# Reordering the ScalarE work of a ramp phase: log/exp of the third unit before the exponentials of the second

## The chip, the cores and the metric

The kernel runs on one core of a Trainium2 chip. The metric is the device time of one execution in microseconds (us). A program on one core has no second die to compare with, so a run is called slow only when it is more than 1.5% above the fastest run of the same kernel.

Engines are named as the profile names them: PE is TensorE (PEld is its weight load), ACT is ScalarE, DVE is VectorE, POOL is GpSimd. "Clock" is the clock that was granted to TensorE: 1.0 is full, 0.5 is half.

## The reference

Two operators follow each other. The first is a gated linear recurrence (a complex decay per channel, D = 48, 8 heads, 4 batches, 768 steps), the second a GEGLU layer with a gated residual on the 3072 tokens that result (384 channels, 1536 hidden).

```python
mag = np.sqrt(a_re * a_re + a_im * a_im)
scale = np.minimum(mag, 0.999) / (mag + 1e-06)
a_re_n, a_im_n = (a_re * scale, a_im * scale)
for t in range(S):                      # S_re, S_im: [B, H, D, D]
    new_re = ar * S_re - ai * S_im
    new_im = ar * S_im + ai * S_re
    S_re, S_im = (new_re + kv, new_im)  # kv = outer(k[t], v[t])
    y[:, :, t] = np.einsum('bhd,bhde->bhe', q[:, :, t], S_re)
# ... x = y with the heads side by side
g = x @ w_gate
gelu = 0.5 * g * (1.0 + erf(g * inv_sqrt2))
ffn_out = gelu * (x @ w_val) @ w_out
return x + 1.0 / (1.0 + np.exp(-(x @ w_res))) * ffn_out
```

The kernel does not step through time. It takes the logarithm of the magnitude and the angle of each decay, forms cumulative sums over 128 tokens by matmuls with triangular matrices, turns them into exponentials (E and its inverse Ei) and sines and cosines (CS), multiplies q and k by these, and so turns the recurrence into causal attention over 128-token blocks plus a carried state.

## The kernel before

The 3072 tokens are 12 groups of 256 (4 batches of 3), and the groups form units: [0], [1,2], [3,4], ... The program alternates between a phase x (log/exp, exponentials, arctan, sines, half of the attention) and a phase y (Gelu and the GEGLU matmuls, the other half of the attention). The program puts a table load on ACT where it changes between the log/exp functions, the trigonometric ones and Gelu; the trace of before has 21 such loads of 1.28 us each. The change is in phase x of unit 0. There "the second unit" is g1 = groups 1 and 2, "the third unit" is g2 = groups 3 and 4.

```python
def p1_steps(g):                        # log/exp of one group
    def s0():
        act(out=T["lm", g], in_=T["lm", g], func=AF.Ln)
    def s1():
        T["s", g] = pS.tile([128, W], FP, tag="s", name="s")          # pS: 2 buffers
        act(out=T["s", g], in_=T["lm", g], func=AF.Exp, scale=-1.0)
        nc.vector.tensor_tensor(out=T["th", g], in0=T["s", g], in1=T["th", g], op=OP.mult)
    def s2():
        act(out=T["s", g], in_=T["th", g], func=AF.Square)
    def s3():
        act(out=T["s", g], in_=T["s", g], func=AF.Ln, bias=1.0)
        # ... two DVE updates of lm
    return [s0, s1, s2, s3]

def cs_l(g, c):                         # cumulative sum of log magnitudes
    cs = psM.tile([128, DM], FP, tag="mm", padded_shape=[128, 512], name="csl")   # psM: 4 PSUM slots
    nc.tensor.matmul(out=cs, lhsT=lmat[c], rhs=T["lm", g][:, sl], start=True, stop=True)
    def ex():
        act(out=T["E", g][:, sl], in_=cs, func=AF.Exp)
        act(out=T["Ei", g][:, sl], in_=cs, func=AF.Exp, scale=-1.0)
    return ex

def cs_t(g, c):                         # cumulative sum of the angles
    if c == 0:
        T["fg", g] = pE.tile([128, C * H, 2, D], FP, tag="fg", name="fg")         # pE: 2 buffers
    cs = psM.tile([128, DM], FP, tag="mm", padded_shape=[128, 512], name="cst")
    nc.tensor.matmul(out=cs, lhsT=tmat[c], rhs=th[:, sl], start=True, stop=(s == 0))
    if s > 0:
        nc.tensor.matmul(out=cs, lhsT=ones2pi, rhs=T["P", g], start=False, stop=True)
    # ... fractions r, fg on DVE; p2_sin then makes CS from fg on ACT

def sums(g):                            # decay between groups
    ms = psM.tile([128, H], FP, tag="mm", padded_shape=[128, 512], name="ms")
    two = pS.tile([128, W], FP, tag="s", name="two")
    # ... two = lm of the last half group + lm of this one, each head twice (DVE)
    for h in range(H):
        nc.tensor.matmul(out=ms[0:DD, h:h + 1], lhsT=two[:, h * DD:(h + 1) * DD], rhs=ones1,
                         start=(h == 0), stop=(h == H - 1), skip_group_check=True)
    T["ms", g] = mp.tile([128, H], FP, tag="ms", name="msb")
    nc.vector.tensor_copy(out=T["ms", g][0:DD], in_=ms[0:DD])

def sums_exp(g):
    act(out=M[0:DD], in_=T["ms", g][0:DD], func=AF.Exp)
```

Phase x weaves its lists of steps: every list gets a begin and an end, and the steps are emitted in order of their positions. ACT's table-bound functions keep the order in which they are emitted.

```python
weave((0.0, 0.25, zip_steps([p1(g) for g in g1])), (0.26, 0.3, csls), (0.31, 0.32, sm[0]), (0.35, 0.45, exs),
      (0.4, 0.64, zip_steps([p1(g) for g in g2])), (0.641, 0.642, dec3), (0.645, 0.65, atn[:1]),
      (0.65, 0.66, [call(p1_arctan, g) for g in g1]), (0.67, 0.85, cst), (0.75, 0.8, atn[1:]),
      (0.9, 0.95, sin), (0.96, 0.97, sm[1]), (0.0, 0.5, att))
```

Here `sm[0]` are the sums of the second unit, `exs` its exponentials, `dec3` the exponentials M of the sums, `atn[:1]` the table load for arctan, `sm[1]` the sums of the third unit, and `att` the attention of unit 0.

## Time and profile before

| reading | before |
|---|---|
| time, median of 3 runs | 323.64 us (323.56 to 323.77) |
| span of the profiled run | 322.4 us |
| PE busy over the span | 272.1 us (84%) |
| ACT table load that ends log/exp | starts at 48.05 us |
| angle matmuls (cst) | from 50.24 us to the next instruction of PE at 57.51 us |
| first Gelu | 65.02 us |

These lines are from the page of before. The first gives busy time and share of the span by engine. In the other two each digit is the busy share, or the granted clock, of one fortieth of the span (8.06 us) in tenths.

```profile
PE 272.1 (84%) x2200; PEld 170.5 (53%) x2200; DVE 234.8 (73%) x431; ACT 209.8 (65%) x353; POOL 80.5 (25%) x115
...
PE   0337927789887999789997999998999999899994
...
PEclk9995676959999999999999999999999999999998
```

From the ninth slice on PE is busy for 70% or more of every slice but the last, so most of a delay there should go into the end time. Before that the slices have a different limit, which the timeline shows. The columns of the timeline are: start in us, duration in us, engine, line, operation, out<-in with shapes, number of merged instructions, and in brackets the idle time before it with what ended it. ACT of before:

```profile
36.59 0.49 ACT L124 ACTIVATE E<-csl 128x384 f32<-128x384 f32 x1 [0.91 <-PE csl L212]
...
40.92 0.48 ACT L399 CAST x<-y 128x384 bf16<-128x384 f32 x1 [0.55 <-PE y L396]
...
48.05 1.28 ACT L477 ACT_TABLE_LOAD   x1
...
57.58 0.94 ACT L124 ACTIVATE CS<-fg,hpi 128x768 bf16<-128x768 f32 x1 [5.20 <-DVE fg L246]
...
65.02 0.66 ACT L124 ACTIVATE h<-gp 128x256 bf16<-128x256 f32 x2
```

PE of before, in the same view:

```profile
39.21 1.44 PE L296 MATMUL ms<-ones,two 128*96 128x1 f32 x16
...
40.72 1.50 PE L296 MATMUL ms<-ones,two 128*96 128x1 f32 x16
50.24 1.65 PE L236 MATMUL cst<-ai,lt0b 128*128 128x384 f32 x2 [7.84 <-ACT ai L124]
51.68 1.49 PE L238 MATMUL cst<-P,ones2pi 128*128 128x384 f32 x2
...
57.51 1.44 PE L296 MATMUL ms<-ones,two 128*96 128x1 f32 x16
```

And DVE of before:

```profile
47.13 0.96 DVE L197 SCALAR_TENSOR_TENSOR ar<-s,ar 128x768 f32<-128x768 f32 x1 [1.64 <-ACT s L124]
...
50.54 0.54 DVE L224 TENSOR_TENSOR P<-ai 128x384 f32<-128x384 f32 x1
...
51.94 0.94 DVE L293 TENSOR_TENSOR two<-ar 128x768 f32<-128x768 f32 x1
...
59.53 0.95 DVE L321 TENSOR_TENSOR Q<-CS,qE 128x1536 bf16<-128x1536 bf16 x1
```

Read together, they say what limits the stretch from 36 to 65 us. PE waits 7.84 us for the arctan (`ai`), which follows the table load, which follows the last log/exp work of ACT. Then ACT waits 5.20 us for the angle fractions `fg`, which follow the cst matmuls. The way to an earlier Gelu is an earlier table load, followed by cst matmuls that need not wait for P.

The windows view gives the length of a stretch, the busy time (and number of instructions) of PE, PEld, DVE, ACT and POOL in it, then the granted clock, the DMA share and GB/s. Two stretches of before:

```profile
54.00:58.00 4.00, 4.00 (x18) 2.40 (x16) 3.29 (x8) 0.42 (x1) 0.00 (x0) 0.96 1.62 155
...
66.00:71.00 5.00, 5.00 (x41) 4.18 (x40) 3.07 (x8) 1.74 (x4) 1.03 (x2) 0.50 0.75 146
```

By windows of 0.4 us (all clock times below are read so, and are good to 0.4 us) the clock of before is half from 44.0 to 54.4 us and again from 64.8 to 71.6 us.

### The profile page before, as it was taken

To read this page: it belongs to the slowest core of one execution; us is meant where nothing else is said; L and a number is where in the kernel's file an instruction comes from. 1 tells how busy PE (TensorE), PEld (TensorE's weight loads), DVE (VectorE), ACT (ScalarE), POOL (GpSimd) and SP (SyncE) were. 2 spreads that over 40 slices of the span, in tenths; PEclk is the share of its full clock that TensorE was granted. 3 is DMA by queue.
4 is the path that set the end of the run, shared out by engine and by line. 5 is a ranking of instruction groups with operands and counts; after the bars stand their busy time and mean duration, and the time that the engine had idled before them with its cause. 6 is when DMAs were issued, how large, how long until landed. Compare 5 with 4: busy or idle time off the path is not lost.

```text
span 322.4 us, 5853 instructions
## 1 busy us (share of the span) xinstructions
PE 272.1 (84%) x2200; PEld 170.5 (53%) x2200; DVE 234.8 (73%) x431; ACT 209.8 (65%) x353; POOL 80.5 (25%) x115
## 2 busy tenths in 40 slices
PE   0337927789887999789997999998999999899994
PEld 0116624677543666445664556554656655555682
DVE  2446769968499995599982999974899837864352
ACT  4549684646998557977568976569665683656150
POOL 1206522022040370259020572000630003200220
PEclk9995676959999999999999999999999999999998
DMA  8999999989999995396850595000360003600441
GB/s 159 218 183 181 182 169 165 185 174 180 187 179 186 223 160 33 76 197 113 122 36 2 107 121 95 2 0 3 75 122 3 2 0 76 122 2 0 107 91 50
DMA packets 137755, 34.55 MB, mean 107 GB/s; under 512 B 126848, under 2 KB 137728, under 8 KB 137728
## 3 DMA queue, kind: packets, MB, share of 16 engines
q1 hardware_dynamic: 103296, 23.60, 36.8%
q0 software_dynamic: 34432, 10.59, 31.2%
q8 instruction: 17, 0.28, 0.3%
q14 instruction: 10, 0.08, 0.1%
HBM read 31.31 MB, written 9.07 MB: 125 GB/s over the span
## 4 chain that ended last, share of the span: by engine, by line
PE 56%; SPq 12%; ACT 11%; DMA 9%; DVE 6%; issue 3%; POOL 1%; ACTq 0%; DVEq 0%; POOLq 0%
PE vp L443 14%; PE gp L439 13%; SPq L136 6%; SPq L144 6%; PE op L463 6%; DMA k<-in_k_dram 4%; PE rp L455 3%; PE tp L349 3%; PE tp L346 3%; PE at L356 3%; ACT L477 3%; DMA m<-dm 3%; ACT s L124 3%; PE cst L236 2%; PE y L394 2%
## 5 line engine op out<-in xcount | busy, mean ns | idle before, releaser
L124 ACT ACTIVATE h<-gp 128x512 bf16<-128x512 f32 (+1 forms) x84 | 44.5, 536 | 38.4 <-PE gp L439 37.9
L439 PE MATMUL gp<-xT,wg 128*128 128x512 bf16 (+1 forms) x252 | 65.4, 353 | 3.4 <-ACT h L124 2.0
L443 PE MATMUL vp<-xT,wv 128*128 128x512 bf16 (+1 forms) x252 | 66.6, 353 | 0.0
L446 DVE SCALAR_TENSOR_TENSOR h<-h,vp 128x512 bf16<-128x512 bf16 (+1 forms) x84 | 49.8, 603 | 16.4 <-PE vp L443 12.0
L463 PE MATMUL op<-wo,h 128*128 128x384 bf16 x288 | 50.2, 326 | 8.1 <-ACT Ei L124 5.9
L463 PEld LDWEIGHTS <-h 128*128 128x128 bf16 x288 | 27.8, 98 | 28.7 <-issue 11.3
L351 ACT COPY qk<-tp 96x512 bf16<-96x512 bf16 x48 | 27.9, 580 | 17.1 <-PE tp L349 7.9
L359 DVE TENSOR_TENSOR atm<-at,mask 128x512 bf16<-128x512 f32 x48 | 32.9, 686 | 8.2 <-PE at L356 7.8
L472 POOL DMA_DIRECT2D out_dram<-x x22 | 20.4, 947 | 54.4 <-DMA out_dram<-ot 43.1
L439 PEld LDWEIGHTS <-wg 128*128 128x128 bf16 x252 | 23.7, 99 | 17.9 <-issue 4.2
L443 PEld LDWEIGHTS <-wv 128*128 128x128 bf16 x252 | 23.8, 99 | 13.3
L189 DVE TENSOR_TENSOR ai<-s,ai 128x768 f32<-128x768 f32 x12 | 11.1, 955 | 23.6 <-ACT s L124 23.6
L477 ACT ACT_TABLE_LOAD x21 | 26.9, 1283 | 1.1 <-PEq L615 0.7
L346 PE MATMUL tp<-ident,Q 128*96 128x128 bf16 x192 | 20.1, 231 | 6.9 <-DVE Q L321 6.2
L346 PEld LDWEIGHTS <-Q 128*96 128x96 bf16 x192 | 17.4, 130 | 15.3 <-DVE Q L321 10.0
L124 ACT ACTIVATE CS<-fg,hpi 128x768 bf16<-128x768 f32 x12 | 11.2, 935 | 20.8 <-DVE fg L246 20.7
L150 POOL DMA_DIRECT2D v<-in_v_dram x24 | 21.9, 932 | 4.2 <-DMA v<-in_v_dram 1.3
L349 PE MATMUL tp<-ident,K 128*96 128x128 bf16 x192 | 22.3, 235 | 0.0
L236 PE MATMUL cst<-ai,lt0b 128*128 128x384 f32 x24 | 11.8, 577 | 11.7 <-ACT ai L124 11.0
L352 DVE COPY qk<-tp 96x512 bf16<-96x512 bf16 x48 | 19.8, 413 | 2.3 <-ACT qk L351 1.7
L212 PE MATMUL csl<-ar,lt0a 128*128 128x384 f32 x24 | 11.4, 562 | 10.8 <-DMA ar<-in_a_re_dram 10.8
L466 DVE SCALAR_TENSOR_TENSOR ot<-sg,op 128x384 f32<-128x384 f32 x24 | 13.1, 547 | 10.1 <-PE op L463 10.1
(85 smaller groups left out, 522.0 us busy)
## 6 DMA issues: line engine op xcount, KB each, us to landing
ar<-in_a_re_dram SPq DMA_DIRECT2D x24, 192.0 KB, 4.7
ai<-in_a_im_dram SPq DMA_DIRECT2D x24, 192.0 KB, 4.1
q<-in_q_dram SPq DMA_DIRECT2D x24, 192.0 KB, 3.8
k<-in_k_dram SPq DMA_DIRECT2D x24, 192.0 KB, 3.7
out_dram<-ot SPq DMA_DIRECT2D x24, 192.0 KB, 2.5
out_dram<-x POOLq DMA_DIRECT2D x22, 192.0 KB, 3.7
v<-in_v_dram POOLq DMA_DIRECT2D x24, 96.0 KB, 5.0
wg<-in_moe_w_gate_dram POOLq DMA_DIRECT2D x4, 288.0 KB, 11.4
```

Of the source, the lines that this page charges most:

```text
L124: tab(nc.scalar.activation(**kw))
L150: nc.gpsimd.dma_start(out=t[:, c], in_=rows(v, g, c))
L346: nc.tensor.transpose(out=tp[0:DD, j * 128:j * 128 + 128], in_=Q(x), identity=ident)
L349: nc.tensor.transpose(out=tp[0:DD, 512 + j * 128:640 + j * 128], in_=K(x), identity=ident)
L351: nc.scalar.copy(out=qk[0:DD, 0:512], in_=tp[0:DD, 0:512])
L359: nc.vector.tensor_tensor(out=atm, in0=at, in1=mask4, op=OP.mult)
L439: nc.tensor.matmul(out=gp, lhsT=wg[:, fi, ffi * 128:(ffi + 1) * 128], rhs=xT[:, fi, :], start=(fi == 0), stop=(fi == KD - 1))
L443: nc.tensor.matmul(out=vp, lhsT=wv[:, fi, ffi * 128:(ffi + 1) * 128], rhs=xT[:, fi, :], start=(fi == 0), stop=(fi == KD - 1))
L446: nc.vector.scalar_tensor_tensor(out=h2[:, ffi, :], in0=h2[:, ffi, :], scalar=0.5, in1=vp, op0=OP.mult, op1=OP.mult)
L463: nc.tensor.matmul(out=ps, lhsT=h2[:, ffi, jj * 128:(jj + 1) * 128], rhs=wo[:, ffi, :], start=(ffi == 0), stop=(ffi == KF - 1))
L472: nc.gpsimd.dma_start(out=out[t0:t0 + 128, :], in_=T["x", token(u, jj)], accum_op=OP.add)
L477: tab(nc.scalar.preload_act_table_set(nm))
```

## The change

The intent is to let ACT start the third unit's log/exp chain (Ln, Exp, Square, Ln, with a DVE product in the middle) before the second unit's eight exponentials, so that the exponentials fill the waits for DVE and the last Ln is reached sooner. No instruction is added or removed.

`two` must leave the ring "s". Otherwise the third unit's Exp would need a buffer that is held by `two`, which is read by matmuls that wait for a PSUM slot, which is freed by exponentials that now stand behind that Exp on ACT. (This is read from the code.) It goes to the ring "fg" of pE, which has two buffers and is otherwise used for the angle fractions.

```diff
-        two = pS.tile([128, W], FP, tag="s", name="two")
+        two = pE.tile([128, C * H, 2, D], FP, tag="fg", name="two").rearrange("p x u d -> p (x u d)")[:, 0:W]
@@
-            weave((0.0, 0.25, zip_steps([p1(g) for g in g1])), (0.26, 0.3, csls), (0.31, 0.32, sm[0]), (0.35, 0.45, exs),
-                  (0.4, 0.64, zip_steps([p1(g) for g in g2])), (0.641, 0.642, dec3), (0.645, 0.65, atn[:1]),
+            p12 = zip_steps([p1(g) for g in g2])
+            weave((0.0, 0.25, zip_steps([p1(g) for g in g1])), (0.26, 0.3, csls), (0.31, 0.32, sm[0]), (0.32, 0.5, p12[:-2]),
+                  (0.5, 0.58, exs), (0.6, 0.64, p12[-2:]), (0.641, 0.642, dec3), (0.645, 0.65, atn[:1]),
```

## The prediction

> **What bounds the kernel now.** On the whole PE: 272 us busy of 322 (84%), and from 72 us on TensorE is 88 to 100% busy in most 8-us windows. The change touches only the ramp's phase from about 23 to 65 us, where PE is not the limit: in the timeline it is idle from 42.4 to 50.2 us (7.84 us, "released by ACT ai"). The limit there is a loop ACT -> DVE -> ACT -> PE: exponentials 36.6 to 42.2, log/exp of the third unit interleaved and ended at 47.8, table load 48.05 (1.28 us), arctan 49.34, cumulative-sum matmuls 50.24 to 57.5, sines 57.6 to 62.7, first Gelu at 65.0. ACT's waits between 32.6 and 48.05 add up to only about 4 us.
>
> **What the change does.** It adds and removes no work, only order and a buffer.
> 1. ACT: two Ln (0.84 us), two Exp, two Square go ahead of the eight exponentials E/Ei (0.48 us each, 0.38 apart). The Ln fill the 0.84-us and 0.5-us waits after 32.6. But both squares wait for DVE's two products, which stand behind attention and sum instructions to about 41.3, so some waits only move. By the durations of the trace I get the table load at about 47.2 instead of 48.05: 0.8 to 1.1 us earlier.
> 2. DVE: the E/Ei now end near 45.3 instead of 42.2. The ones-column sums (ms) wait for PSUM buffers that E/Ei free, so they start near 43 instead of 39.2; the copies msb, qE, xT and kE stand behind them on DVE, and behind these the log-magnitude updates and the carry P. I expect that update at 47.5 to 48.6 instead of 47.13, P at 51 to 52 instead of 50.54, and the second sum matmul, which needs P, at 51.5 to 52.6 instead of 51.68. That eats the gain of step 1.
> 3. The buffer of "two" moves from the s ring to the fg ring (else the Exp of the third unit would wait for sums that wait for exponentials behind it on ACT). So the third "two" must wait for both sines of the first group (to about 59.4), and TensorE's ms behind it, then gate/value matmuls, Q, K. I expect Q 1 to 3 us later than 59.5, K likewise, first Gelu 64 to 67 (before 65.02).
> 4. TensorE clock. The windows view shows 0.5 from 44 to 54 and from 64.6 to 71.3 us, in steps of about 3.4 us; matmuls there take twice as long. [...] With sums and gate/value matmuls moved later, the slow stretch around 64.6 can shift, shorten or lengthen: an estimated -2 to +1.5 us.
>
> **Sum.** Steps 1 to 3: first Gelu from -1 to +2 us, mid +0.8. Step 4: mid -0.6. What is left at 72 us goes through nearly whole, because PE is dense afterwards. I predict 323.8 us, 322.2 to 325.8 for 8 in 10. Over 2% either way would need 6.5 us: 1% each.
>
> **What would show it.** Step 1: last table load before arctan starts at 47 to 47.5. Step 2: ms starts after 42.5; DVE's first update of the third unit not before 47.3; idle of PE before the second sum matmul. Step 3: "two" in the 58-to-61 stretch with ACT CS as its releaser, and ms behind it. Step 4: the windows view of granted clock from 54 to 74.
>
> **What would make it wrong.** The clock staying full from 54 us on (then 321 to 322); the sums not delaying DVE because the clock is still full at 43 to 46; or the delayed Q and K of the second unit cascading through attention into the following phase (then 326).

+0.8 us for steps 1 to 3 and -0.6 us for step 4 on the 323.63 us of before give the 323.8 us. The -2 to +1.5 us of step 4 is the estimate for the slow stretch that the windows view shows there (0.5 from 64.6 to 71.3 us, in steps of about 3.4 us), not a measured figure. That matmuls take about twice as long there can be read from PE's records of before: cst matmuls start 640 ns apart at half clock (51.0 to 54.2 us) and 322 to 323 ns apart at full clock (54.6 to 57.2 us).

## The result

| reading | before | changed |
|---|---|---|
| time, median of 4 runs | 323.63 us (323.56 to 323.77) | 327.41 us (326.99 to 328.52) |
| span of the profiled run | 322.4 us | 325.1 us |
| ratio of fast runs | 1 | 1.0122 (95%: 1.0094 to 1.0149) |

A ratio is the mean time of one kernel's fast runs over the mean of the other's of the same rounds, so it is not quite the ratio of the medians in the table. The changed kernel is slower, by less than 2%. The same kernel was measured again later, on the second of the three chips of the experiments, where it was 0.7% slower (below). The page of the changed kernel:

```profile
PE 274.0 (84%) x2175; PEld 173.8 (53%) x2200; DVE 233.9 (72%) x431; ACT 209.3 (64%) x353; POOL 80.3 (25%) x115
...
PE   0336876699977999789998899998989999899995
...
PEclk9955655859999999999999999999999999999999
```

The busy times are within 2 us of those of before, PEld's within 3.3 us (25 of PE's records are missing in this trace). The work is the same; it stands later. ACT of the changed kernel:

```profile
39.66 0.48 ACT L399 CAST x<-y 128x384 bf16<-128x384 f32 x1 [3.30 <-PE y L396]
...
41.91 0.47 ACT L124 ACTIVATE E<-csl 128x384 f32<-128x384 f32 x1
...
48.74 0.21 ACT L124 ACTIVATE M<-msb 96x8 f32<-96x8 f32 x1 [2.16 <-DVE msb L299]
48.96 1.28 ACT L477 ACT_TABLE_LOAD   x1
...
60.69 0.94 ACT L124 ACTIVATE CS<-fg,hpi 128x768 bf16<-128x768 f32 x1 [7.39 <-DVE fg L246]
...
68.88 0.66 ACT L124 ACTIVATE h<-gp 128x256 bf16<-128x256 f32 x2
```

PE of the changed kernel:

```profile
42.81 2.72 PE L296 MATMUL ms<-ones,two 128*96 128x1 f32 x16 [3.19 <-ACT Ei L124]
45.78 2.72 PE L296 MATMUL ms<-ones,two 128*96 128x1 f32 x16 [0.25 <-DVE msb L299]
...
51.15 1.65 PE L236 MATMUL cst<-ai,lt0b 128*128 128x384 f32 x2 [2.31 <-ACT ai L124]
53.56 1.65 PE L238 MATMUL cst<-P,ones2pi 128*128 128x384 f32 x2 [0.77 <-DVE P L224]
...
60.08 0.81 PE L238 MATMUL cst<-P,ones2pi 128*128 128x384 f32 x2
...
63.50 1.49 PE L296 MATMUL ms<-ones,two 128*96 128x1 f32 x16 [2.61 <-DVE two L293]
```

DVE of the changed kernel:

```profile
48.54 0.16 DVE L299 COPY msb<-ms 96x8 f32<-96x8 f32 x1 [1.91 <-PE ms L296]
...
50.02 0.95 DVE L197 SCALAR_TENSOR_TENSOR ar<-s,ar 128x768 f32<-128x768 f32 x1
...
52.96 0.55 DVE L224 TENSOR_TENSOR P<-ai 128x384 f32<-128x384 f32 x1
...
62.39 0.96 DVE L293 TENSOR_TENSOR two<-ar 128x768 f32<-128x768 f32 x1 [0.21 <-ACT CS L124]
...
65.11 0.94 DVE L321 TENSOR_TENSOR Q<-CS,qE 128x1536 bf16<-128x1536 bf16 x1
```

And the same two stretches in the windows view:

```profile
54.00:58.00 4.00, 4.00 (x7) 2.08 (x7) 2.31 (x5) 0.00 (x0) 0.00 (x0) 0.50 1.52 152
...
66.00:71.00 5.00, 4.36 (x36) 3.71 (x35) 4.35 (x8) 2.35 (x5) 1.93 (x3) 0.50 0.99 193
```

The reader should follow one chain through these lines.

1. The sums `ms` need a PSUM slot that an exponential frees. The exponentials now start at 41.91 instead of 36.59 us, so the first sum starts at 42.81 instead of 39.21 us ("3.19 <-ACT Ei").
2. By then the clock is half (0.50 in the windows view from 42.0 us). Sixteen one-column matmuls take 2.72 instead of 1.44 us. The second sum starts only when DVE has copied out the first ("0.25 <-DVE msb"); it seems to get the first one's PSUM slot. The second copy is done at 48.70 us.
3. M, the exponential of the sums, stands ahead of the table load on ACT. It waits 2.16 us for that copy, and the table load behind it starts at 48.96 instead of 48.05 us. ACT was otherwise idle for these 2.16 us, and the load did not pass.
4. DVE's updates and P stand behind the same copy. P starts at 52.96 instead of 50.54 us, and the second cst matmul waits for it (0.77 us).
5. The clock stays half until 58.8 instead of 54.4 us.

The cst matmuls therefore end 3.2 us later. Their end is read as the start of the next instruction that was ready: PE's `ms` at 57.51 us of before; in the changed kernel the last two start at 60.08 us, and two such matmuls take 0.65 us at full clock (pairs of before start at 54.93, 55.57, 56.22 and 56.86 us), which gives 60.73 us. This delay of 3.22 us has three terms: the first cst matmul is 0.91 us later (51.15 - 50.24); from the first to the second it took 2.41 instead of 1.44 us, which is 0.97 us for P; and the rest, 1.34 us, is the longer half-clock stretch (without the wait, the eight matmuls took 8.61 instead of 7.27 us).

Then the buffer comes in. The third unit's `two` waits in the fg ring for the sines (62.39 instead of 51.94 us), PE is idle for 2.61 us before its sums, and Q is at 65.11 instead of 59.53 us. The first Gelu is 3.86 us later (68.88 instead of 65.02), the table load that ends the next phase y 3.1 us later (86.61 instead of 83.52), and the whole span 2.7 us longer.

### The profile page after: what moved, and what is told of

The parts are those of the page before. It is cut to its first block, busy times and chain, and to the rows that moved or that the text cites. A ratio compares the mean times of both kernels' runs of the same rounds, so it can differ in the third digit from the quotient of the medians.

```text
span 325.1 us, 5825 instructions
## 1 busy us (share of the span) xinstructions
PE 274.0 (84%) x2175; PEld 173.8 (53%) x2200; DVE 233.9 (72%) x431; ACT 209.3 (64%) x353; POOL 80.3 (25%) x115
## 4 chain that ended last, share of the span: by engine, by line
PE 48%; SPq 15%; DMA 12%; ACT 10%; DVE 8%; issue 4%; POOL 1%; ACTq 0%; DVEq 0%; POOLq 0%
PE gp L439 12%; PE vp L443 12%; SPq L136 10%; PE op L463 5%; SPq L144 5%; DMA q<-in_q_dram 4%; PE rp L455 4%; ACT s L124 3%; PE tp L346 3%; PE tp L349 3%; DMA m<-dm 3%; PE at L356 3%; ACT L477 2%; PE y L394 2%; PE dk L386 2%
## 5 line engine op out<-in xcount | busy, mean ns | idle before, releaser
L439 PE MATMUL gp<-xT,wg 128*128 128x512 bf16 (+1 forms) x241 | 63.7, 352 | 2.9 <-DVE xT L430 1.2
L443 PE MATMUL vp<-xT,wv 128*128 128x512 bf16 (+1 forms) x238 | 61.8, 350 | 0.3
L359 DVE TENSOR_TENSOR atm<-at,mask 128x512 bf16<-128x512 f32 x48 | 33.0, 687 | 10.4 <-PE at L356 9.9
L472 POOL DMA_DIRECT2D out_dram<-x x22 | 20.0, 928 | 54.8 <-DMA out_dram<-ot 54.4
L477 ACT ACT_TABLE_LOAD x21 | 26.9, 1283 | 1.1 <-PEq L616 0.7
L394 PEld LDWEIGHTS <-atm 128*128 128x128 bf16 x192 | 12.6, 97 | 14.1 <-DVE atm L359 12.7
```

The source lines that it names most:

```text
L359: nc.vector.tensor_tensor(out=atm, in0=at, in1=mask4, op=OP.mult)
L439: nc.tensor.matmul(out=gp, lhsT=wg[:, fi, ffi * 128:(ffi + 1) * 128], rhs=xT[:, fi, :], start=(fi == 0), stop=(fi == KD - 1))
L443: nc.tensor.matmul(out=vp, lhsT=wv[:, fi, ffi * 128:(ffi + 1) * 128], rhs=xT[:, fi, :], start=(fi == 0), stop=(fi == KD - 1))
L477: tab(nc.scalar.preload_act_table_set(nm))
```

## The experiments

Four theories stood at the start or came up on the way. The expectations call them by these letters or by their content.

- A: the loss comes from the sums, which stand behind the exponentials through the PSUM slots and hold back M, the table load and P.
- B: the loss comes from the buffer: the third unit's `two` waits for the sines in the fg ring.
- C: the loss, or its size, comes from TensorE's clock.
- D: the loss lies in ACT's order itself: with the exponentials moved away, ACT idles 3.3 us for the last attention block, and what it then does stands in a row.

Twelve runs of ten kernels were made on three chips, each beside the kernel before. All gave correct results. A trace shows one execution and not always a typical one: the traces of the sums in slots of their own, the milder order and the idle matmuls before the cst matmuls are of the slowest execution of their kernels, those of the buffer alone on the first chip, the idle matmuls in the second stretch and the last kernel are of the fastest.

### First chip: each part of the change alone

Four kernels, three rounds. The kernel before scattered more here than in any other round: 323.5 to 327.0 us in seven runs, median 324.23. The times decide little, and the traces were used instead.

**The buffer alone**, in the order of before.

```diff
 # on before
-        two = pS.tile([128, W], FP, tag="s", name="two")
+        two = pE.tile([128, C * H, 2, D], FP, tag="fg", name="two").rearrange("p x u d -> p (x u d)")[:, 0:W]
```

> The kernel before (old order of ACT) with only the buffer part of the change: all three 'two' tiles from the fg ring. Theory B (the new wait of the third 'two' for both sines of the first group, with the ms sums, gate/value matmuls, Q and K behind it, costs time by itself): the third 'two' starts near 59.3 us, released by ACT CS, first Q near 61.9 instead of 59.5, first Gelu near 66.5 instead of 65.0, time 325 to 326.5 us. Theory A (the loss comes from the sums that wait for PSUM slots behind the exponentials): no such wait here, time 323.4 to 324.2 us, as before.

Measured: median 325.27 us, ratio 1.0005 (0.9942 to 1.0069; one run of 328.7 us was slow and is left out of the ratio), profiled span 321.8 us. The wait appeared as theory B says. In the timeline of this kernel:

```profile
59.53 0.96 DVE L293 TENSOR_TENSOR two<-ar 128x768 f32<-128x768 f32 x1 [0.21 <-ACT CS L124]
```

`two` came 7.6 us later than before, Q at 62.61 instead of 59.53 us, the first Gelu at 66.38 instead of 65.02 us. Yet the span did not grow, because the second half-clock stretch was only one step long in this execution, 61.6 to 65.2 us. The delay was there, and the shorter stretch made up for it.

**The order alone**: the changed kernel, with the third unit's `two` in a tile that is free at that time.

```diff
 # on the changed kernel
-        two = pE.tile([128, C * H, 2, D], FP, tag="fg", name="two").rearrange(...)[:, 0:W]
+        two = (hb.tile([128, 4, DM], FP, tag="sg", name="two").rearrange("p j d -> p (j d)")[:, 0:W]
+               if g > UNITS[1][-1] else
+               pE.tile([128, C * H, 2, D], FP, tag="fg", name="two").rearrange(...)[:, 0:W])
```

> The changed kernel, but the third 'two' in a tile that nobody else uses then (the sg tile), so it no longer waits for the sines; order of ACT as changed. Theory A: sums still start after 42.5 us and run at half clock, table load near 49, cumulative-sum matmuls end near 60.5, first Gelu 67 to 67.5, time 325.3 to 326.5 us. Theory B: time back to 323.0 to 324.0 us, as before.

Measured: median 326.06 us, ratio 1.0039 (0.9988 to 1.0089), span 324.0 us. Its DVE lines:

```profile
54.32 0.95 DVE L293 TENSOR_TENSOR two<-ar 128x768 f32<-128x768 f32 x1
...
62.80 0.94 DVE L321 TENSOR_TENSOR Q<-CS,qE 128x1536 bf16<-128x1536 bf16 x1
```

The wait of `two` is gone, and Q comes 2.3 us earlier than in the changed kernel, but the first Gelu only 0.6 us earlier (68.29). The sums still start at 42.76 and 45.73 us and take 2.72 us each. So most of the delay at the first Gelu is there without the buffer's wait: theory B alone is not enough.

**The sums in PSUM slots of their own**, to take their wait for the exponentials away.

```diff
 # on the changed kernel
-        ms = psM.tile([128, H], FP, tag="mm", padded_shape=[128, 512], name="ms")
+        ms = (psY if g % 2 else psA).tile([128, H], FP, tag="y" if g % 2 else "at",
+                                          padded_shape=[128, 512], name="ms")
```

> The changed kernel, but the ms sums take the PSUM slots of attention (at and y), so they wait for no exponential; the 'two' tiles stay in the fg ring. Theory A: sums run near 39 to 42 us, M waits for nothing, table load 46.5 to 47.5, P near 50.5, time 324.5 to 326 us (what is left is theory B's wait). Theory B: P earlier but the third 'two' still behind the sines: 326.5 us or more.

Measured: median 325.38 us, ratio 1.0019 (0.9962 to 1.0076), span 325.3 us. This run did not test what it was made for. The slots are those of the attention's `y` and `at`, so the scheduler put the sums ahead of the last `y` on PE; ACT then waited 6.33 us for `y` and the table load came at 50.40 us, later than in the changed kernel. One wait was exchanged for another.

**Both of these.** The edit is the sum of the last two.

> Both: sums in attention's PSUM slots and the third 'two' outside the fg ring. If A and B together are all of the loss, the gain that was intended shows: table load 46.5 to 47.5 us (48.05 before), first Gelu 64 to 65, time 322.3 to 323.4 us. If the reordering of ACT itself is at fault (theory D: ACT waits 3.3 us for the last attention cast and the products), 324.5 us or more.

Measured: median 325.19 us, ratio 1.0021 (0.9972 to 1.007), span 323.5 us. ACT's lines:

```profile
42.77 0.48 ACT L399 CAST x<-y 128x384 bf16<-128x384 f32 x1 [6.33 <-PE y L396]
...
49.42 1.28 ACT L477 ACT_TABLE_LOAD   x1
```

The gain that A and B together promised did not come. With sums and buffer set free, ACT still reaches the table load late, since it has nothing to do while it waits for `y`: the exponentials that had filled this time stand behind. That brought up theory D. But this is no clean test of D either: the wait for `y` is 6.33 us here and 3.30 us in the changed kernel, because the sums again stand ahead of `y` on PE (from 39.09 us, `y` from 41.93). Without these 3.03 us the table load would come at an estimated 46.4 us. The order has to be tested with less of it moved.

### Second chip: the parts again with five rounds, and a milder order

Before: median 323.85 us, 11 runs from 323.24 to 325.39.

**The changed kernel again.** No edit.

> The changed kernel again, in the same rounds as the parts of it below, because single runs scattered by 2 us. Theories A and B: 326 to 328.5 us against 323.5 to 324.5 for before in the same rounds.

Measured: median 326.55 us, ratio 1.0068 (1.0033 to 1.0104), span 324.9 us. The slowdown is confirmed, at roughly half the size of the first measurement. The half-clock stretches were 45.2 to 58.8 and 65.6 to 72.4 us, so the first and long one is there again, but it began later, and the first sum ran at full clock:

```profile
43.44 1.52 PE L296 MATMUL ms<-ones,two 128*96 128x1 f32 x16 [3.47 <-ACT Ei L124]
```

```profile
48.17 0.21 ACT L124 ACTIVATE M<-msb 96x8 f32<-96x8 f32 x1 [0.96 <-DVE msb L299]
48.39 1.28 ACT L477 ACT_TABLE_LOAD   x1
```

M still waits for the sums, 0.96 instead of 2.16 us, and the table load is 0.34 us later than before, P 1.85 us (52.39). (The exponentials are 0.63 us later in this execution, at 42.54 us.) So with one of the two sums at full clock the late sums still hold back both; the half clock adds to the wait.

**The buffer alone again.** No further edit.

> Old order of ACT with the three 'two' tiles in the fg ring (buffer part alone), more rounds. Theory B, if the ring's wait is worth something by itself: 0.8 to 2 us over before. Theory C (the clock): the delayed Q and K are partly paid back by another place of the slow-clock stretch, so 0 to 0.8 us over before on average, with a scatter of 2 us or more.

Measured: median 326.11 us, ratio 1.0054 (1.0022 to 1.0085), one run slow and left out, span 323.9 us. The trace agrees with that of the first chip until 61.6 us. Then the second half-clock stretch lasts three steps (61.6 to 72.0 us) instead of one. The windows view of the two executions of this one program, the first chip's first:

```profile
66.00:71.00 5.00, 4.31 (x59) 3.66 (x59) 5.00 (x12) 2.77 (x7) 0.27 (x2) 1.00 0.84 164
```

```profile
66.00:71.00 5.00, 4.36 (x37) 3.76 (x36) 3.42 (x7) 2.07 (x6) 2.03 (x3) 0.50 1.02 201
```

In the same 5 us PE did 59 matmuls at full clock and 37 at half clock. The end of the next phase y (its closing table load) is at 82.93 and 85.46 us, and the times of the two profiled executions are 323.60 and 325.80 us. So the length of this one stretch is worth 2.2 us, in a program that did not change. That is theory C, as a source of scatter as large as the effect under study. (They ran on two chips, so a part of the chip's own in the 2.2 us is not excluded.)

**The order alone again.** No further edit.

> New order of ACT, third 'two' in the sg tile (order part alone), more rounds. Theory A (late sums): 1.5 to 2.5 us over before, and most of the loss of the changed kernel. Theory B: under 0.7 us over before.

Measured: median 325.81 us, ratio 1.0048 (1.0019 to 1.0078), span 323.7 us, first Gelu 68.08 us. On this chip, then, with the ratio less one times the mean of before (324.21 us): order alone +1.6 us, buffer alone +1.8 us, both +2.2 us. Each part costs, and they do not add up: where the order has made everything late, the buffer's wait is partly hidden behind it. The intervals are about 1 us wide to each side, so the split between the parts is rough.

**A milder order**: only the first half of the third unit's chain (two Ln, two Exp) ahead of the exponentials, and the free tile for `two`.

```diff
 # on the order-alone kernel
-  (0.32, 0.5, p12[:-2]), (0.5, 0.58, exs), (0.6, 0.64, p12[-2:])
+  (0.32, 0.41, p12[:4]), (0.41, 0.5, exs), (0.5, 0.64, p12[4:])
```

> As a_two, but the exponentials E/Ei go between the third unit's Exp and its Square, so ACT does not stand idle for the last attention cast and the products, and the sums get their PSUM slots early. Theory A and D (loss = sums late and ACT idle 3.3 us before the cast): table load at 45.3 to 46.5 us (48.05 before, 48.96 changed), first Gelu 62.5 to 64.5, time 321.5 to 323.0 us, better than before. If instead the order in the ramp is worth nothing because later work waits for something else: within 0.5 us of before.

Measured: median 322.81 us, ratio 0.9959 (0.993 to 0.9988), span 322.2 us. Faster than before, but the table load came at 47.63 us and not at the 45.3 to 46.5 that was expected. ACT shows why:

```profile
43.38 0.84 ACT L124 ACTIVATE s<-ai 128x768 f32<-128x768 f32 x1 [0.41 <-DVE ai L189]
45.10 0.84 ACT L124 ACTIVATE s<-ai 128x768 f32<-128x768 f32 x1 [0.88 <-DMA k<-in_k_dram]
```

Both squares wait for DVE's products. The second line names a DMA as its releaser, but the square reads the product, and in the timeline of DVE each product starts right behind a copy `msb` of the sums: the copies start at 42.28 and 43.93 us, after waits of 1.83 and 0.58 us for PE's sums, and the products at 42.39 and 44.11 us. So with the order mended, the sums' place on DVE is what is left of theory A.

### Third chip: clock and place of the sums

Before: median 324.20 us, 11 runs from 323.49 to 325.14. Five rounds.

**Idle matmuls before the cst matmuls**, to end the first half-clock stretch sooner.

```diff
 # on the changed kernel
+    def warm(n, lhsT, rhs):
+        wm = psY.tile([128, 512], FP, tag="y", name="wm")
+        for _ in range(n):
+            nc.tensor.matmul(out=wm[:, 0:rhs.shape[-1]], lhsT=lhsT, rhs=rhs, start=True, stop=True)
@@
+            wst = [lambda: warm(2, lmat[1], T["s", g2[0]][:, 0:DM])]
-                  (0.9, 0.95, sin), (0.96, 0.97, sm[1]), (0.0, 0.5, att))
+                  (0.641, 0.642, wst), (0.9, 0.95, sin), (0.96, 0.97, sm[1]), (0.0, 0.5, att))
```

> The changed kernel plus two idle fp32 matmuls on TensorE (result unused) that wait for the third unit's Ln and so run in the idle stretch before the cumulative-sum matmuls; nothing else moves. Theory C (part of the loss is TensorE at half clock, 1.3 us in the cumulative sums): the clock is full from about 52 us instead of 58.8, these matmuls end 1.5 to 3 us earlier (near 58 instead of 60.7), first Gelu near 66.5, ratio to before 1.000 to 1.005 instead of 1.007. If the clock is only a bystander: the ratio stays at 1.006 or more.

Measured: median 325.29 us, ratio 1.004 (1.0012 to 1.0067), span 324.8 us. PE's lines:

```profile
48.80 2.87 PE L511 MATMUL wm<-s,ut0a 128*128 128x384 f32 x4
...
57.89 0.81 PE L238 MATMUL cst<-P,ones2pi 128*128 128x384 f32 x2
...
61.52 2.07 PE L296 MATMUL ms<-ones,two 128*96 128x1 f32 x16 [2.83 <-DVE two L293]
```

The clock was full from 52.0 us, and the last cst matmuls started 2.2 us earlier than in the changed kernel (57.89 instead of 60.08). Of this 0.8 us was left at the first Gelu (68.11), since the second half-clock stretch now lasted from 62.4 to 72.4 us. The third `two` still cost 2.83 us. So the first stretch is a real part of the delay of the cst matmuls. The first Gelu was expected near 66.5 us, and that did not come: in this execution the second stretch began 3.2 us sooner than in the changed kernel and lasted one step of 3.4 us longer. By the times it is not shown that these idle matmuls help: the interval overlaps that of the changed kernel on the second chip (1.0033 to 1.0104).

**Idle matmuls in the second stretch**, in the kernel before, with nothing else changed: three beside the first Q and three beside the first K.

```diff
 # on before, with the same warm()
         pr = [st for g in gs(u + 1) for st in products(g)]
+        if u == 0:
+            fl = lambda t: t.rearrange("p x u d -> p (x u d)")[:, 0:512]
+            pr.insert(2, lambda: warm(3, ident, fl(T["Q", gs(1)[0]])))
+            pr.insert(5, lambda: warm(3, ident, fl(T["K", gs(1)[0]])))
```

> The kernel before plus six idle bf16 matmuls of 512 columns at the start of the second unit's attention, three behind Q's transposes and three behind K's, in TensorE's idle gaps of 60.9 to 63.3 us; nothing else moves. Theory C: the half-clock stretch of 64.8 to 71.6 us does not come, time 1 to 2.5 us under before and less scatter between runs. If the stretch comes all the same or its clock is not limiting: within 0.5 us of before.

Measured: median 322.48 us, ratio 0.9951 (0.9929 to 0.9973), span 320.1 us. The windows view of this kernel, where before had 0.50:

```profile
66.00:71.00 5.00, 4.92 (x74) 4.27 (x72) 4.79 (x12) 3.06 (x8) 2.09 (x3) 1.00 0.90 171
```

The first Gelu is where it was (64.95 us against 65.02), the half-clock stretch after it is gone, and the end of the next phase y comes 2.7 us earlier (80.83 instead of 83.52). Six extra matmuls that compute nothing made the kernel 0.5% faster.

**The sums after both products**: the milder order, with the sums of the second unit emitted later, behind the third unit's two products on DVE.

```diff
 # on the milder order
-  (0.31, 0.32, sm[0])
+  (0.405, 0.406, sm[0])
```

> As a_split, with the sums of the second unit placed after the third unit's products on DVE (there ACT waited 0.41 and 0.88 us for these products behind the sums' copies). Theory A and D: table load at 46.2 to 46.8 instead of 47.63, time 0.5 to 1.2 us under a_split, that is a ratio to before of 0.992 to 0.995. If DVE's later sums come back as a wait for P: no better than a_split (0.996).

Measured: median 320.64 us (320.54 to 323.58), ratio 0.9909 (0.9876 to 0.9941), span 319.4 us. Its PE sums, and ACT's table load:

```profile
40.67 2.85 PE L296 MATMUL ms<-ones,two 128*96 128x1 f32 x32 [1.07 <-DVE two L293]
```

```profile
44.79 1.28 ACT L477 ACT_TABLE_LOAD   x1
```

Both sums run in one go, at full clock and without a wait for each other, in 2.85 us. They start 1.46 us later than before (39.21), but their last copy starts at 43.56 us, ahead of M's turn on ACT at 44.46: what counts is not that they are early, but that nothing waits for them. The table load comes 3.26 us earlier than before (46.2 to 46.8 was expected), the first Gelu at 61.81 us (3.21 us earlier), and the span is 3.0 us shorter. This is the gain that the change was after.

**This and the six idle matmuls** of the kernel above.

> sp_sm0 with the six idle matmuls of b_w2o. Theory C: no half-clock stretch in 63 to 72 us, another 1 to 2 us, ratio to before 0.985 to 0.992.

Measured: median 320.82 us (318.4 to 322.36), ratio 0.9889 (0.9851 to 0.9928), span 316.5 us. The second half-clock stretch is gone in the trace, and the profiled span is 2.9 us shorter than without the idle matmuls, but this is the fastest execution of this kernel beside the second slowest of the other. The intervals of the two ratios overlap widely, so by times it is open whether the matmuls add anything here. Both kernels beat the one before and the changed one.

## Why the prediction was wrong

The measured 327.41 us lies 1.6 us above the upper end of the range, 325.8. "Within 2%" was right. Measured again on the second chip the same kernel gave 326.55 us, also above. Point by point:

**"I get the table load at about 47.2 instead of 48.05" (step 1): wrong in sign.** It came at 48.96 us. The step counted ACT's own work and its wait for the products. It left out that M stands between the last Ln and the table load on ACT, and that M needs the sums, which step 2 of the same prediction had already moved later. The two steps were costed as if the sums delayed DVE alone. The timeline shows M waiting 2.16 us. Without this wait the load would have come at 46.80 us (48.96 - 2.16), 47.43 in the second measurement (48.39 - 0.96), so the sum of ACT's own work was about right; the missing wait is the step that failed. With the sums set right and less of the order changed, the table load was at 44.79 us, so the direction of the idea was sound.

**"I expect that update at 47.5 to 48.6, P at 51 to 52, the second sum matmul at 51.5 to 52.6" (step 2): mechanism right, size too small.** Measured were 50.02, 52.96 and 53.56 us. The start of the sums was right ("near 43"; 42.81 us). The prediction knew that the clock could be half there, but its figures leave no room for two sums of 2.72 instead of 1.44 us one after the other, nor for the second one's wait for the copy of the first; together these put the last copy at 48.54 us instead of 42.25.

**"I expect Q 1 to 3 us later than 59.5, first Gelu 64 to 67" (step 3): mechanism right, size too small.** `two` waits for the sines and PE waits 2.61 us for it, as predicted, but it adds to a sine that is itself 3.1 us late: Q came 5.6 us later and the Gelu at 68.88 us. The buffer alone put Q 3.1 us later, which is about the predicted 1 to 3; the rest is the order.

**"Step 4: mid -0.6" (clock): wrong in sign.** The slow stretch around 65 us kept its length (64.8 to 71.6, then 65.6 to 72.4). The stretch before it grew from 10.4 us (44.0 to 54.4) to 17.2 us (41.6 to 58.8), right across the cst matmuls, at a cost of 1.34 us. The prediction looked for a shift in the wrong stretch.

**"What is left at 72 us goes through nearly whole": about right.** From 3.86 us at the first Gelu 3.1 us were left at the end of phase y and 2.7 us at the end.

**"What would make it wrong": the third guess was close.** It named the delayed Q and K cascading into the following phase, with 326 us. That is part of what happened, but the delay began earlier, at the sums.

What stays open: the first measurement gave +1.2% and the second +0.7%, with intervals that overlap only a little, and the lengths of half-clock stretches differ from one execution to the next. How much of that difference is the clock and how much the chip was not measured. No run set the sums free without moving something else, so theory A's share alone is read from the traces and not measured. For D the runs show a gain that the change gave away (with less moved the load comes earlier than before), but not that ACT's own order made the load late: without M's wait it would have come before 48.05 us.

## What to carry to other kernels

Before moving work on an engine whose trace shows one instruction waiting behind another, as the table load did behind M here (2.16 us), list what stands between the moved work and its goal, and where each of those inputs comes from: here a tiny exponential that needed a two-step sum held back the table load. A wait that one sees in an engine can be filled by work that does not itself wait; moving half of the chain did that (ratio 0.9959), moving all of it emptied the engine elsewhere (ratio 1.0048 with the order alone; in the changed kernel ACT idled 3.30 us before the last attention cast). Where a trace shows TensorE's clock at half, as here from 44.0 to 54.4 and from 64.8 to 71.6 us of before, compare the half-clock windows of both traces before explaining a difference of half a per cent, since two executions of one program differed by 2.2 us with them.

## What the traces show of the clock and of the loads

- The clock records of before have two values in the ramp, 1.0 and 0.5, and lie 3.413, 13.653, 6.827 and 10.24 us apart: the longer ones are two to four times the shortest. In before, 2.04 us of PE work in 3.30 us (61.4 to 64.7 us, transposes and matmuls of 48 and 128 columns) were followed by half clock; with the idle 512-column bf16 matmuls, 2.82 us of work in the same stretch were followed by full clock. Busy time alone does not separate the cases: in the kernel with the sums after both products PE was busy for 2.97 of the 3.41 us before the clock fell (at 44.15 us by its clock records), 2.78 us of it with the one-column sums. What decides it was not shown: no run here varied the kind of work alone.
- Weight loads of 96 float32 columns start 85 ns apart at full clock (before, 39.2 to 42.2 us) and 160 ns apart at half clock (changed kernel, 42.8 to 48.4 us). (A single load is recorded as 165 and 280 ns, but neighbouring loads overlap.) Sixteen in a row at these distances make the one-column sums 1.44 or 2.72 us long.
- The length of one half-clock stretch went with a difference of 2.2 us of 324 between two executions of one program, which is 0.7%, and that is as large as the effects studied here: removing one half-clock stretch with idle matmuls gave a ratio of 0.9951.
- All 21 table loads of before take 1283 ns. The one before arctan starts at 48.05 us, 0.02 us after M ends (47.74 + 0.29), and the next activation starts at 49.34 us, 1.29 us after the load's start.
